# Storing the small gate rows of an mLSTM kernel from another engine's queue

## The chip, the cores and the metric

The kernel runs on one core of a Trainium2 chip. The time is device time of one execution in microseconds (us). The kernel before took 461.69 us, the median of three runs (461.58 to 464.37). The engines are named PE (TensorE, matrix products; PEld is its weight load), DVE (VectorE), ACT (ScalarE), POOL (GpSimd) and SP (SyncE, which only issues transfers). ScalarE and GpSimd can issue transfers too; a queue is named SPq or ACTq after its engine.

## The reference

An mLSTM cell over batch 4, 8 heads, 768 time steps and head size 40, whose output, read as 3072 tokens of 320, goes through an up product, a sigmoid-GELU and a down product.

```python
for t in range(S):
    m_new = np.maximum(f_gate[:, :, t] + m, i_gate[:, :, t])
    f_stab = np.exp(f_gate[:, :, t] + m - m_new)
    i_stab = np.exp(i_gate[:, :, t] - m_new)
    m = m_new
    C = f_stab * C + i_stab * outer(v_t, k_t)
    n = f_stab * n + i_stab * k_t
    y[:, :, t] = sigmoid(o_gate[:, :, t]) * (C @ q_t) / np.maximum(np.abs(n @ q_t), 1.0)
...
h = x @ w_in                                   # x: (3072, 320), w_in: (320, 2048)
g = h * (1.0 / (1.0 + np.exp(-1.702 * h)))
out = (g @ w_out).astype(np.float32)           # w_out: (2048, 320)
```

## The kernel before, in words

The sequence is cut into six chunks `w` of 128 steps. Within a chunk the recurrence is unrolled into attention-like products over 128 x 128 masked weights, plus a state that is carried from chunk to chunk. The program writes out the order of every engine by hand; each engine runs its instructions in that order and waits by semaphores.

From the second chunk on (`w` = 1 to 5) a chunk has two stages. In the first product, `up_fast(w, j)` for j = 0 to 7, a pair of the 16 column blocks of `w_in` is multiplied with the chunk's tokens: a Strassen-like scheme of seven products per pair, some of them shared through row banks. TensorE writes into four PSUM banks that `ps_m` hands out in turn and into the two double banks `p_a0` and `p_a1`. ScalarE copies one product to `parts` (L768), applies the activation to the pair before (L697) and copies one row bank to `g` (L746); VectorE adds up the rest (L769, L770, L782, L783); GpSimd adds the last part (L789). In the second product, `down_fast`, 14 blocks of products are multiplied with `w_out`, and between them stand the attention steps of chunk `w + 1`, at places given by the table `at` in `attention`: `columns`, `scale`, `decay`, `weights`, `carry` (the state, from k and v), `scores`, `values` and the `seam` steps, which bring the result into token order by way of memory.

The work around the change prepares chunk `w + 1` during the first product of chunk `w`:

- `load_squares` (L108), issued near the end of the second product before: k and q in square order, eight transfers by SyncE, 2.6 MB.
- `gates(w + 1)` behind the first pair (j = 0), on VectorE: the running sum of the forget gate (`f_run`), the running maximum (`m_run`), the stacked and swapped rows (`swapped`, in the tile named `f_run`) and the chunk's two decay ends (`both`). SyncE stores them to memory: three transfers to `m_row` (L304, L307), one to `st_row` (L330), one to `d_row` (L331). For `w + 1` = 1 it is GpSimd's queue instead, which `side_queue` chooses.
- `load(w + 1, "o")` (L122): the output gate into `eo`, 640 KB.
- `columns_in(w + 1)` behind the third pair (j = 2): SyncE reads the stored rows back in another layout into `raw` (four transfers from `st_row`, L354, and one from `d_row`, L356). `spread(w + 1)` reads `m_row` back to every partition into `wt` (L407). `load(w + 1, "vk")` (L120) loads v and k, three transfers each.
- `columns_turn` (behind the last pair) and the attention steps use `raw`, `wt`, `v_st` and `k_st`.

All these transfers of SyncE stand in one queue in the order given, and a store waits there until VectorE has made its rows. The `seam_out` stores of the second half are issued by ScalarE (L560). The row tiles in memory have two buffers, `m_run`, `swapped` and `st` have one.

Of the kernel before, what the change touches and what calls it, by code (L numbers as in the profile page):

```python
# [8 lines left out]
FP = mybir.dt.float32  # L9
# [17 lines left out]
def kernel(  # L27
# [14 lines left out]
    BH = B * H  # L42
# [10 lines left out]
    HL = L // 2  # L53
# [11 lines left out]
    rows = ctx.enter_context(tc.tile_pool(name="rows", bufs=2, space=bass.MemoryType.DRAM))  # L65
# [4 lines left out]
    V, A, G, T = nc.vector, nc.scalar, nc.gpsimd, nc.tensor  # L70
# [154 lines left out]
    m_at, ends = {0: m0}, {}  # L225
    cols, stacked, m_row, raw = {}, {}, {}, {}
# [51 lines left out]
    def side_queue(w):  # L278

        return G if w == 1 else nc.sync  # L280

    def gates(w):
        m = m_at[w]
        swapped = gate.tile([3 * BH, L], FP, bufs=1, name="f_run")
        f_run = swapped[0:BH, :]
        m_run = gate.tile([BH, L], FP, bufs=1, name="m_run")
        st = stacked[w] = gate.tile([3 * BH, L], FP, bufs=1, name="st")
        V.tensor_tensor_scan(out=f_run, data0=ones, data1=f_sb[w], initial=0.0, op0=OP.mult, op1=OP.add)
        a = st[0:BH, :]
        V.tensor_tensor(out=a, in0=i_sb[w], in1=f_run, op=OP.subtract)  # L290
        if w == 0:
            room = work.tile([L, H, D1], FP, tag="u", name="room").rearrange("p h d -> p (h d)")
            neg, part = room[0:BH, 0:L], room.bitcast(BF)[0:BH, 2 * L:3 * L]
            V.tensor_tensor(out=neg, in0=f_run, in1=i_sb[w], op=OP.subtract)
            split(G, a3, neg, neg, part)
        V.tensor_tensor_scan(out=m_run, data0=ones, data1=a, initial=m, op0=OP.mult, op1=OP.max)
        if w == 0:

            room = work.tile([L, H, D1], FP, tag="u", name="room").rearrange("p h d -> p (h d)")
            left, part = room[0:BH, 0:L], room.bitcast(BF)[0:BH, 2 * L:3 * L]  # L300
            split(V, m3, m_run, left, part)
        else:
            to = m_row[w] = rows.tile([2, BH, HL], FP, name="m_row")
            side_queue(w).dma_start(out=to[:, 0::2].rearrange("n h t -> h n t"),  # L304
                              in_=m_run[0::2].rearrange("h (n t) -> h n t", t=HL))
            for n in range(2):
                side_queue(w).dma_start(out=to[1 - n, 1::2], in_=m_run[1::2, n * HL:(n + 1) * HL])  # L307
        end = m_run[:, L - 1:L]
        if w + 1 < NW:
            m_at[w + 1] = gate.tile([BH, 1], FP, name="m_end")  # L310
            V.tensor_tensor(out=m_at[w + 1], in0=f_run[:, L - 1:L], in1=end, op=OP.add)

        mid = m_run[:, HL - 1:HL]
        for x, (old, new) in enumerate(((m, mid), (mid, end)) if w else ((m, end),)):
            t = slice(x * HL, x * HL + HL) if w else slice(0, L)
            V.tensor_scalar(out=st[BH:2 * BH, t], in0=m_run[:, t], scalar1=old, scalar2=None, op0=OP.subtract)
            V.tensor_scalar(out=st[2 * BH:3 * BH, t], in0=a[:, t], scalar1=new, scalar2=-1.0, op0=OP.subtract,
                            op1=OP.mult)
        if w:
            for x in range(2):  # L320
                V.tensor_scalar(out=swapped[:, x * HL:(x + 1) * HL], in0=st[:, (1 - x) * HL:(2 - x) * HL], scalar1=odd,
                                scalar2=None, op0=OP.mult)
            V.scalar_tensor_tensor(out=swapped, in0=st, scalar=even, in1=swapped, op0=OP.mult, op1=OP.add)
            both = ends[w] = gate.tile([BH, 2], FP, name="both")
            V.tensor_tensor(out=both[:, 0:1], in0=m, in1=mid, op=OP.subtract)
            V.tensor_tensor(out=both[:, 1:2], in0=mid, in1=end, op=OP.subtract)
            st_row = rows.tile([L // 32, 3 * BH, 32], FP, name="st_row")
            d_row = rows.tile([BH, 2], FP, name="d_row")
            stacked[w] = st_row, d_row
            side_queue(w).dma_start(out=st_row.rearrange("n k t -> k n t"), in_=swapped.rearrange("k (n t) -> k n t", t=32))  # L330
            side_queue(w).dma_start(out=d_row, in_=both)  # L331

    def slot(i, x):

# [23 lines left out]
    def columns_turn(w):  # L358
        c = cols[w] = gate.tile([L, 4 * BH], FP, name="cols")
        V.transpose(out=c[:, 0:3 * BH].rearrange("p (k h) -> p k h", h=BH),  # L360
                    in_=raw[w][:, 0:3 * BH].rearrange("p (k t) -> p k t", t=32))
# [232 lines left out]
    def wait_for(x):  # L594

        G.tensor_copy(out=mark[0:x.shape[0]], in_=x[:, 0:1])
# [212 lines left out]
    def weight_sums(n):  # L809
        out, a, b = ((t1, w01, w00), (t2, w11, t1), (w01, w11, w01), (t4, w10, t2))[n]  # L810
        G.tensor_tensor(out=out, in0=a, in1=b, op=OP.subtract)
# [60 lines left out]
    def run(calls):  # L872
        for f, *args in calls:
            f(*args)
# [62 lines left out]
    for w in range(NW):  # L937
        more = w + 1 < NW
        if w == 0:
            for j in range(NF // 2):  # L940
                if j % 2 == 0:
                    ahead, behind = converted[j // 2]
                    run([(convert, p) for p in ahead] + [(fetch, p) for p in fetched.get(j // 2, ())])
                    up(w, j, lambda: run([(columns_turn, 1) if p is None else (convert, p) for p in behind]))
                if j == 6:
                    load(1, "o")
                if j == 1:
                    wait_for(w_in_sb[:, 1, 512:1024])
                    scale(0, 1)
                    load(1, "v")  # L950
                if j < B and j % 2:
                    carry(0, (j // 2,))
                if j == 3:
                    masks()
                    gates(1)
                    columns_in(1)
                if j == 4:
                    spread(1)
                    load_squares(1, "q")
                if j >= B:  # L960
                    transposes(1, j - B)
        else:
            token_sums(w)
            for j in range(NF // 2):
                up_fast(w, j)
                if more and j == 0:
                    gates(w + 1)
                    load(w + 1, "o")
                    if w == 1:
                        wait_for(ends[w + 1])  # L970
                if w == 1 and j < 2:
                    weight_sums(j + 2)
                if more and j == 2:
                    columns_in(w + 1)
                    spread(w + 1)
                    load(w + 1, "vk")
                if more and j:
                    for n in ((0, 2), (), (4,), (6, 1, 3), (5, 7), (), ())[j - 1]:
                        block_transposes(w + 1, n)
                if more and j == 7:  # L980
                    columns_turn(w + 1)
                if 2 <= j < 6:
                    hidden_difference(w, j - 2)
                if j >= 6:
                    hidden_sums(w, (j - 6,), G)
            gelu_fast(w, NF // 2 - 1)
            hidden_sums(w, (2, 3), V)
        side = attention(w + 1) if more else {}
        if w == 0:

            blocks = [(lambda b=b, n=n: down(w, b, n)) for n0 in (0, 2) for b in range(B) for n in (n0, n0 + 1)]
        else:
            blocks = down_fast(w, 0) + down_fast(w, 1)
        for i, block in enumerate(blocks):
            if w == 0 and i in (0, 4, 5):
                convert((17, 18, 19)[max(i - 3, 0)])
            if w + 2 < NW and i == (6 if w == 0 else 0):
                load_gates(w + 2)
            if w + 2 < NW and i == 13:
                load_squares(w + 2, "kq" if w else "k")  # L1000
            if w == 0 and i == 15:
                load_squares(w + 2, "q")
            block()
            run(side.get(i, []))
            if w == 0 and i == 3:
                for n in (1, 3, 5, 7):
                    block_transposes(1, n)
            if w == 0 and i == 6:
                wait_for(wt[1, 0][:, 0, 0, :])
                weight_sums(0)  # L1010
                weight_sums(1)
            if w == 0 and i in (11, 13):
                input_sums(slice(0, 4) if i == 11 else slice(4, 8))
# [30 lines left out]
```

## Time and profile before

| | |
|---|---|
| median of three runs | 461.69 us |
| profiled execution | 463.3 us, of which span 461.6 us |
| granted TensorE clock | 1.000 |
| first products of `w` = 1 to 5 start at | about 112, 182, 254, 325, 396 us |
| second products of `w` = 1 to 5 start at | about 143, 214, 286, 357, 428 us |
| busy in 254 to 286 us (first product, `w` = 3) | PE 32.0, DVE 27.7, ACT 14.5, POOL 15.1; DMA share 0.91 |
| busy in 286 to 325 us (second product, `w` = 3) | PE 38.8, DVE 29.9, ACT 12.7, POOL 11.6; DMA share 0.39 |
| share of the chain that ended last | PE 75%, DVE 11%, ACT 4%, SPq 4%, DMA 3% |

"L304" is line 304 of the kernel. In a timeline a row has start and length in us, engine, line, operation, the tile written and the tile read, and the number of instructions merged; in brackets stands the idle time before it and what ended it. For transfers the length is that of the issue on its queue, not of the transfer; the time to landing is given apart. The DMA share is the mean busy share of the core's 16 DMA engines, and can go above 1 where packets overlap.

### The profile page before, as it was taken

How to read it: one execution, taken by the hardware profiler on the slowest of the kernel's cores; microseconds unless marked ns; L12 is line 12 of the kernel's file. 1: busy time of each engine (PE TensorE's matmuls, PEld its weight loads, DVE VectorE, ACT ScalarE, POOL GpSimd, SP SyncE). 2: the span in 40 equal slices, each digit the busy share in tenths (PEclk: the TensorE clock that was granted, in tenths of full speed). 3: DMA queues.
4: the chain of work that ended last, by engine and by line, in shares of the span. 5: the costliest groups of instructions: out<-in, count | busy, mean ns of one | idle time of the engine just before them, and what ended most of it. 6: DMA issues, size and time to landing. Idle time of an engine off the chain costs nothing.

```text
span 461.6 us, 12375 instructions
## 1 busy us (share of the span) xinstructions
PE 452.8 (98%) x5071; PEld 386.5 (84%) x5071; DVE 350.9 (76%) x738; ACT 186.0 (40%) x433; POOL 162.7 (35%) x155
## 2 busy tenths in 40 slices
PE   8999999999999999999899999999999999999996
PEld 6777877775779999779899779999888999787996
DVE  6788998899988876889786888787788767554622
ACT  5686779100546600546700354900264810164100
POOL 5101318130677500266700167610157710146200
PEclk9999999999999999999999999999999999999999
DMA  8999999038969044959224979315989505000000
GB/s 165 186 289 195 251 234 221 5 67 186 179 138 122 3 102 115 193 79 174 36 61 109 195 117 165 50 37 122 176 130 156 76 18 141 28 1 1 1 28 30
DMA packets 135561, 52.87 MB, mean 115 GB/s; under 512 B 101984, under 2 KB 131632, under 8 KB 135504
## 3 DMA queue, kind: packets, MB, share of 16 engines
q1 hardware_dynamic: 127136, 50.27, 56.0%
q10 hardware_dynamic: 8048, 1.66, 1.8%
q8 instruction: 40, 0.66, 0.7%
q0 software_dynamic: 320, 0.15, 0.2%
q14 instruction: 17, 0.14, 0.1%
HBM read 44.52 MB, written 7.54 MB: 113 GB/s over the span
## 4 chain that ended last, share of the span: by engine, by line
PE 75%; DVE 11%; ACT 4%; SPq 4%; DMA 3%; issue 2%; DVEq 0%; ACTq 0%
PE p_out L852 30%; PE p_h L729 16%; PE p_a L729 6%; PE p_h L631 5%; PE p_h L708 4%; PE p_a L708 3%; SPq L120 2%; PE p_a L507 2%; DMA st_row<-f_run 2%; PE p_a L515 2%; PE p_a L463 2%; PE p_a L605 2%; ACT wt L439 2%; PE p_h L640 1%; PE p_a L390 1%
## 5 line engine op out<-in xcount | busy, mean ns | idle before, releaser
L789 POOL TENSOR_TENSOR g<-g,parts 128x512 f32<-128x512 f32 x30 | 38.2, 1274 | 184.7 <-ACT g L746 175.9
L768 ACT COPY parts<-p_h 128x256 f32<-128x256 f32 x40 | 14.9, 372 | 164.6 <-PE p_h L729 159.5
L852 PE MATMUL p_out<-w_out_sb,g 128*128 128x160 f32 x480 | 68.9, 300 | 0.0
L852 PEld LDWEIGHTS p_out<-w_out_sb,g 128*128 128x128 f32 x480 | 66.4, 190 | 0.5
L697 ACT ACTIVATE g<-g 128x512 f32<-128x512 f32 x80 | 47.7, 629 | 23.8 <-DVE g L783 18.8
L857 DVE TENSOR_TENSOR o_sb<-o_sb,p_out 128x160 f32<-128x160 f32 x70 | 21.4, 317 | 43.6 <-PE p_out L852 43.0
L852 PE MATMUL p_out<-t_sb,s 128*128 128x160 f32 x320 | 47.1, 300 | 0.0
L729 PE MATMUL p_h<-xT,w_in_sb 128*128 128x256 f32 x160 | 45.4, 386 | 0.0
L852 PEld LDWEIGHTS p_out<-t_sb,s 128*128 128x128 f32 x320 | 44.4, 190 | 0.2
L729 PE MATMUL p_h<-t_x,s_in 128*128 128x256 f32 x160 | 41.2, 380 | 0.2 <-DVE t_x L684 0.2
L439 ACT ACTIVATE wt<-wt,cols 128x64 f32<-128x64 f32 x160 | 38.8, 333 | 0.1
L729 PEld LDWEIGHTS p_h<-xT,w_in_sb 128*128 128x128 f32 x160 | 29.4, 190 | 9.8 <-issue 6.3
L798 PE MATMUL p_out<-w_out_sb,g 128*128 128x320 f32 x128 | 35.7, 436 | 0.0
L729 PEld LDWEIGHTS p_h<-t_x,s_in 128*128 128x128 f32 x160 | 30.2, 190 | 4.8 <-DVE t_x L684 0.6
L798 PEld LDWEIGHTS p_out<-w_out_sb,g 128*128 128x128 f32 x128 | 23.9, 190 | 9.6
L769 DVE TENSOR_TENSOR t_x<-p_h,parts 128x256 f32<-128x256 f32 x40 | 17.0, 425 | 16.8 <-ACT g L697 8.7
L631 PE MATMUL p_h<-xT,w_in_sb 128*128 128x256 f32 x128 | 29.6, 384 | 0.0
L631 PEld LDWEIGHTS p_h<-xT,w_in_sb 128*128 128x128 f32 x128 | 23.6, 190 | 5.3 <-issue 2.4
L820 POOL TENSOR_TENSOR g<-g 128x512 f32<-128x512 f32 x20 | 25.5, 1276 | 0.0
L443 POOL TENSOR_SCALAR_AFFINE_SELECT wt<-wt 64x1024 f32<-64x1024 f32 x20 | 23.4, 1170 | 5.4 <-ACT wt L439 4.7
L852 PE MATMUL p_out<-w_out_sb,s 128*128 128x160 f32 x160 | 23.8, 302 | 0.0
L852 PE MATMUL p_out<-t_sb,g 128*128 128x160 f32 x160 | 23.8, 302 | 0.0
(221 smaller groups left out, 892.4 us busy)
## 6 DMA issues: line engine op xcount, KB each, us to landing
q_sq<-in_q_dram SPq DMA_DIRECT2D x20, 320.0 KB, 10.2
wt<-m_row SPq DMA_DIRECT2D x20, 256.0 KB, 5.6
k_sq<-in_k_dram SPq DMA_DIRECT2D x16, 320.0 KB, 6.3
out_dram<-o_sb SPq DMA_DIRECT2D x24, 160.0 KB, 1.9
eo<-in_o_gate_dram SPq DMA_DIRECT2D x5, 640.0 KB, 8.5
bits<-in_moe_w_in_dram SPq DMA_DIRECT2D x6, 512.0 KB, 11.4
q_sq<-x_row SPq DMA_DIRECT2D x10, 256.0 KB, 2.9
v_st<-in_v_dram SPq DMA_DIRECT2D x14, 160.0 KB, 5.9
```

Source lines behind the costliest of these rows:

```text
L439: A.activation(out=x[:, h, :], in_=x[:, h, :], func=AF.Exp, scale=-1.0, bias=cols[w][:, c * PH + h:c * PH + h + 1])
L443: G.affine_select(out=r, in_=r, compare_op=OP.is_ge, fill=0.0, base=0, pattern=[[0, PH], [1, HL]], channel_multiplier=-1)
L631: T.matmul(ph[j][i][:, t], w_in_sb[:, c, f * 128:(f + 1) * 128], x[:, c, t], start=(first and c == 0 and n == 0), stop=(not first and c == ...
L697: A.activation(out=gs[w, j][:, i, :], in_=gs[w, j][:, i, :], func=AF.Gelu_apprx_sigmoid)
L708: T.matmul(row[:, t], w_in_x[r, j, :], xT[w][r, 2].rearrange("p b t -> p (b t)")[:, t], start=(start and h == 0), stop=(not start and h == ...
L729: T.matmul(out, a, x[n], start=start, stop=stop)
L769: V.tensor_tensor(out=u2, in0=p56[:, right], in1=y[:, left], op=OP.add)
L789: G.tensor_tensor(out=g0, in0=g0, in1=u, op=OP.add)
L798: T.matmul(po, gs[w, f // 2][:, f % 2, b * L:(b + 1) * L], w_out_sb[:, f, :], start=(f == 0), stop=(f == NF - 1))
L820: G.tensor_tensor(out=a10, in0=a00, in1=a10, op=OP.subtract)
L852: T.matmul(po, a(f), b[:, f, :], start=(f == 0), stop=(f == NH - 1))
L857: V.tensor_tensor(out=dst, in0=x, in1=po, op=OP.add)
```

## The change

From `w + 1` = 2 on, the five stores of the small rows are no longer issued by SyncE inside `gates`, behind the first pair (j = 0). The tiles are kept in `held`, and a new function `gates_out` issues the five stores from ScalarE behind `up_fast(w, 1)`, the second pair, ahead of the read-back, which stays on SyncE behind the third pair. The data, the layouts and the number of transfers stay as they were; for `w + 1` = 1 the stores stay with GpSimd.

```diff
+    held = {}
+
+    def maxima_out(w, m_run, engine):
+        to = m_row[w]
+        engine.dma_start(out=to[:, 0::2].rearrange("n h t -> h n t"), in_=m_run[0::2].rearrange("h (n t) -> h n t", t=HL))
+        for n in range(2):
+            engine.dma_start(out=to[1 - n, 1::2], in_=m_run[1::2, n * HL:(n + 1) * HL])
+
+    def columns_out(w, swapped, engine):
+        st_row, d_row = stacked[w]
+        engine.dma_start(out=st_row.rearrange("n k t -> k n t"), in_=swapped.rearrange("k (n t) -> k n t", t=32))
+        engine.dma_start(out=d_row, in_=ends[w])
+
+    def gates_out(w):
+        m_run, swapped = held[w]
+        maxima_out(w, m_run, A)
+        columns_out(w, swapped, A)
+
     def gates(w):
...
-            to = m_row[w] = rows.tile([2, BH, HL], FP, name="m_row")
-            side_queue(w).dma_start(out=to[:, 0::2].rearrange("n h t -> h n t"),
-                              in_=m_run[0::2].rearrange("h (n t) -> h n t", t=HL))
-            for n in range(2):
-                side_queue(w).dma_start(out=to[1 - n, 1::2], in_=m_run[1::2, n * HL:(n + 1) * HL])
+            m_row[w] = rows.tile([2, BH, HL], FP, name="m_row")
+            if w == 1:
+                maxima_out(w, m_run, G)
...
-            side_queue(w).dma_start(out=st_row.rearrange("n k t -> k n t"), in_=swapped.rearrange("k (n t) -> k n t", t=32))
-            side_queue(w).dma_start(out=d_row, in_=both)
+            if w == 1:
+                columns_out(w, swapped, G)
+            held[w] = m_run, swapped
...
                 if w == 1 and j < 2:
                     weight_sums(j + 2)
+                if more and j == 1:
+                    gates_out(w + 1)
                 if more and j == 2:
                     columns_in(w + 1)
                     spread(w + 1)
```

## The prediction, made before the changed kernel ran

> **What bounds the kernel now.** I read the busy times first, then what TensorE waits for, then the chain of waits in order of time from 182 us on, then SyncE's queue and ScalarE's order of time around the stores that move.
>
> ```profile
> PE 452.8 (98%) x5071; PEld 386.5 (84%) x5071; DVE 350.9 (76%) x738; ACT 186.0 (40%) x433; POOL 162.7 (35%) x155
> ```
>
> TensorE is busy 452.8 of 461.6 us. Of the 8.8 us left, 5.6 lie between 22 and 460 us (busy 432.44 of 438.00). No edit to transfers can win more than that. Its own waits, of which these two can be traced to a transfer:
>
> ```profile
> PE p_a L605 <- DMA k_st<-in_k_dram: 0.6, 1, 0.6
> PE p_a L463 <- DVE state L616: 0.6, 1, 0.6
> ```
>
> Both lie in one place, at 223.0 and 228.5 us, in the second product of the chunk that starts at 182 us. The chain of waits (start, length, what) leads from there back to a store that moves:
>
> ```profile
> 192.29 9.55 DMA st_row<-f_run
> ...
> 201.91 1.86 SPq L354
> ...
> 209.03 4.51 SPq L120
> ...
> 219.41 4.12 DMA k_st<-in_k_dram
> ```
>
> The stacked rows need 9.55 us to land; only then does SyncE issue their read-back, the spread of the maxima, v and k, and TensorE's `carry` meets the last piece of k at 223.57. SyncE's queue ahead of that (start, length, issues):
>
> ```profile
> 180.88 2.08 SPq L108 DMA_DIRECT2D k_sq<-in_k_dram  x4
> 183.06 5.59 SPq L108 DMA_DIRECT2D q_sq<-in_q_dram  x4
> 188.74 1.48 SPq L861 DMA_DIRECT2D out_dram<-o_sb  x1
> 190.32 0.61 SPq L304 DMA_DIRECT2D m_row<-m_run  x1
> 190.98 1.22 SPq L307 DMA_DIRECT2D m_row<-m_run  x2
> 192.29 0.53 SPq L330 DMA_DIRECT2D st_row<-f_run  x1
> 194.05 0.32 SPq L331 DMA_DIRECT2D d_row<-both  x1
> 196.66 0.40 SPq L122 DMA_DIRECT2D eo<-in_o_gate_dram  x1
> ```
>
> Two gaps matter, before `d_row` and before `eo`. SyncE's waits put both down to `q_sq` loads (L331 3.7 us over 4 chunks, L122 9.2 us over 5), whose data neither reads. Counted in this queue, `d_row` is the eighth issue after the second `q_sq` load and `eo` the eighth after the third: an issue waits for the landing of the one eight before it. ScalarE at the point where the stores go (behind the copy at 192.32):
>
> ```profile
> 192.32 0.56 ACT L746 COPY g<-p_h 128x512 f32<-128x512 f32 x1
> 193.90 0.59 ACT L746 COPY g<-p_a 128x512 f32<-128x512 f32 x1 [1.01 <-PE p_a L729]
> 194.38 0.38 ACT L768 COPY parts<-p_h 128x256 f32<-128x256 f32 x1
> 194.65 1.16 ACT L697 ACTIVATE g<-g 128x512 f32<-128x512 f32 x2
> 195.70 0.37 ACT L768 COPY parts<-p_h 128x256 f32<-128x256 f32 x1
> ```
>
> It is idle 1.02 us there (192.88 to 193.90).
>
> **Part 1, what leaves SyncE.** Five issues a chunk in four chunks (those starting at 112, 182, 254, 325 us): 1.92 us for the three `m_row`, 0.58 for `st_row`, 0.37 for `d_row` with their gaps, 2.87 in all. TensorE never waits for these issues as such. `eo` then follows the output store at 190.3 instead of 196.66, its eighth predecessor being a `k_sq` load long landed. `eo` has no reader before 226 us, so that alone is worth nothing.
>
> **Part 2, what ScalarE gets.** The same five issues, behind the second pair. Their data are ready (DVE writes `both` at 191.69, ScalarE arrives at 192.88), so no wait for DVE is added. ScalarE's own issues on its queue, the four `x_row` and `x_rest` stores at 170.59, took 1.40 and 1.08 us for pairs, 0.62 each, so five cost about 2.9, as on SyncE. But `d_row` is now the eighth issue after the third `q_sq` load (q, out, `eo`, three `m_row`, `st_row`, `d_row`), and if ScalarE's issues count with SyncE's it waits for the landing that `eo` waits for today: 123.60, 196.66, 268.22, 339.66 in the four chunks. The trace shows no such wait on ScalarE; its cost is bounded by nothing and by those times. I take the wait, because ScalarE's `x_row` stores each have a semaphore instruction among them beyond their data's.
>
> Behind `d_row` on ScalarE stand the third pair's row copy (L746), its L768 copy, the gelus of the second pair and the fourth pair's L768 copy. That last one frees the PSUM bank into which TensorE multiplies as the second product of the fifth pair. ps_m hands out four banks in turn. In the 182 chunk it ends at 196.07 and TensorE gets there at 198.44, so the cover is 2.37 us, plus ScalarE's 1.02 idle: 3.39 us may pass free. With the row copy at s, the L768 copy ends at s + 2.17. By chunk:
> - 112: ScalarE arrives 121.99, the issues end at 124.86; the copy ends at 127.05 (the GpSimd wait at 124.95 is absorbed), needed at 127.51: no stall.
> - 182: arrives 192.88, `d_row` goes at 196.66 and ends 196.98; copy ends 199.17, needed 198.44: 0.73.
> - 254: arrives 265.04, `d_row` 268.22 to 268.54; copy ends 270.73, needed 270.59: 0.14.
> - 325: arrives 335.98, `d_row` 339.66 to 339.98; copy ends 342.17, needed 341.55: 0.62.
>
> Together 1.5 us. DVE's half of the pair moves with it: its L770 of the fourth pair goes from 198.33 to about 200.7, and TensorE needs that bank at 200.17 plus the 0.73. It fits. DVE's 0.93 us wait for TensorE at 202.3 then takes up most of the delay.
>
> **Part 3, when the rows land.** Now behind 2.6 MB of k and q in one queue; after, in a queue of their own beside them. Nearest rows: ScalarE's stores land in 2.5 to 2.9 us in a quiet stretch, and the first chunk's stores by GpSimd's queue, beside a DMA share of 0.84 to 0.90, in 3.3 (`m_row`), 5.5 (`st_row`) and 6.0 (`d_row`). I take the latter: `st_row` at 194.8 + 5.5 = 200.3 (201.84 now), `d_row` at 202.7, against 205.28 when its read-back is issued now. SyncE's first read-back is stretched to 1.86 us by `eo` draining ahead of it; an earlier `eo` shortens that. So v and k come some 2 to 3 us sooner. Worth: the 0.57 us wait for k, and of the 0.62 us behind it half, since GpSimd's `vw` (220.19, held by v) also starts sooner: 0.9 us, at most 1.2, at least 0. No other chunk has a wait to win.
>
> **Sum.** On the profiled execution (463.3 us, of which 461.6 span): 463.3 - 0.9 + 1.5 = 463.9. It lay 1.6 above the median, 461.69, so 462.3 us.
>
> **A rule against it.** ScalarE and SyncE issued at the same moment at 172.6 us (0.54 and 0.6 us) and at 244.5 (0.56 and 0.62), no longer than either does alone. The Trainium skill, Perfetto Trace Analysis, "DMA Instruction — HWDGE (DVE, Sync)", says that the descriptor generator is shared by two sequencers and locked by one while it generates, and that this lock wait counts in the issue's length. By the rows the five issues keep their 2.9 us and the sum stands at 462.3. By the rule ScalarE's issues could queue behind `eo`'s, and the time would go to that of the second rival, some 482. The rows are of small transfers, so they don't settle it.
>
> **Rivals.**
> 1. *The cover holds*: no landing is waited for on ScalarE, the five issues take 2.9 us, under 3.39, and only the gain is left: 461.69 - 0.9 = 460.8; with the whole 1.2, 460.5, less 0.1 for the distance of the two close runs (461.58 and 461.69) 460.4. For it: the idle time and the L768 slack in every chunk. Against: the two gaps in SyncE's queue.
> 2. *ScalarE is held behind `eo`* (slower). On SyncE the issue after `eo` ends 7.1 us after it (196.66 to 203.77). If that holds another engine's issues too, the first `m_row`, with `eo` issued at 190.3, is done between 197.4 and, counting that q drains until about 197 (the DMA share falls from 1.14 to 0.54 there) and `eo`'s 640 KB follow, 200.5; the five end at 199.7 to 202.8, the L768 copy 2.2 later, 3.5 to 6.6 past TensorE's need. Times four chunks: 14 to 26 us, 476 to 488, middle 482. It decides from 3.39 us of ScalarE's time on. For it: such blocked issues (5.59 us for four, 4.51 for one) stand on SyncE. Against: the two overlaps above.
> 3. *Each issue is slow beside full DMA engines*: at the longest ScalarE issue seen, 0.94 us, five take 4.95 with gaps and the stalls are 1.6 in each chunk, 6.4 in all: 461.69 - 0.9 + 6.4 = 467.2.
> 4. *The rows land later than now*: the transfers stop (DMA share 0.03 or less) about 1 us ahead of `carry` in the 254 chunk (294 against 294.87) and 2 us in the others (150 against 151.79, 364 against 365.84), in the 182 chunk they don't. A read-back 3 us late costs 3 + 2 + 1 + 1 = 7: 468.7. It needs `d_row` to take over 11 us to land, as long as the slowest row store today.
>
> **How the numbers follow.** One per cent, 4.6 us, is about what a measurement of this kernel tells from no change. The forecast, stalls of 0.5 to 3 us against the gain, has 0.47 (own range 461 to 464); rival 1 0.25; rival 2 0.12; rival 3 0.10; rival 4 0.04; a gain over 1%, 0.02, for which the idle of TensorE hardly leaves room. Within 1% stand the first two and the lower end of rival 3: 0.74; slower 0.24. The range takes in the forecast and rivals 1 and 3: 460.4 to 467.5, leaving 0.18 out.
>
> **What would show it.** ScalarE's queue with five issues after the copy at about 192.9 and a gap ahead of the fifth; TensorE idle 0.1 to 0.8 us ahead of the second product of the fifth pair in the chunks at 182, 254 and 325, put down to the L768 copy; `eo` at about 190 and the read-back at about 200; no wait for `k_st` at L605. An `m_row` issue on ScalarE longer than 3 us would make rival 2 right; no idle at the fifth pair, rival 1. The forecast is wrong if the median is below 461 or above 464.

## The result, and the profile after

The changed kernel takes 463.39 us (median of 21 executions, 461.84 to 466.73), the kernel before, run beside it, 462.20 us (median of 21, 461.58 to 464.37). The ratio is 1.0032 with a 95% interval of 1.0020 to 1.0045: slower by 1.2 us between the medians and 1.5 us by the ratio, within one per cent. (In the experiments, too, a ratio is to the kernel before, run beside that version.) The profiled execution of the changed kernel took 463.11 us, of which 461.4 us are span, at a granted clock of 1.00. Lines below the new functions carry numbers 17 higher than before (L463 is now L480, L605 is L622, L746 is L763).

The busy times of the changed kernel, and what its TensorE waits for (us in total, times, longest), answer to the two views shown first:

```profile
PE 453.0 (98%) x5071; PEld 386.7 (84%) x5071; DVE 351.7 (76%) x738; ACT 185.2 (40%) x433; POOL 162.6 (35%) x155
```

```profile
PE p_a L480 <- DVE state L633: 1.0, 1, 1.0
```

The counts of instructions are those of before and each busy time is within 1 us of it, and no wait is put down to an L785 copy (the stall that was forecast) or to `k_st`. ScalarE's timeline in the chunk that starts at 182 us, where the stores now stand:

```profile
191.97 0.64 ACTq L286 DMA_DIRECT2D m_row<-m_run  x1
192.05 0.56 ACT L763 COPY g<-p_h 128x512 f32<-128x512 f32 x1
192.65 1.24 ACTq L288 DMA_DIRECT2D m_row<-m_run  x2
193.99 0.53 ACTq L292 DMA_DIRECT2D st_row<-f_run  x1
194.61 0.44 ACTq L293 DMA_DIRECT2D d_row<-both  x1
195.09 0.59 ACT L763 COPY g<-p_a 128x512 f32<-128x512 f32 x1 [2.48 <-DMA m_row<-m_run]
```

Five issues follow each other without a gap and hold ScalarE until 195.09; `d_row` waits for nothing. All five first products take as long as before, from the first matmul of a stage to the first of the next: 33.67 us in the chunk at 112 us (its first matmul stands at 109.07), 31.84 to 31.88 in the others. SyncE's timeline of the same chunk shows what was not forecast:

```profile
180.61 2.08 SPq L108 DMA_DIRECT2D k_sq<-in_k_dram  x4
182.80 12.96 SPq L108 DMA_DIRECT2D q_sq<-in_q_dram  x4
195.87 0.43 SPq L878 DMA_DIRECT2D out_dram<-o_sb  x1
196.40 0.39 SPq L122 DMA_DIRECT2D eo<-in_o_gate_dram  x1
196.88 8.87 SPq L371 DMA_DIRECT2D raw<-st_row  x4
```

The four `q_sq` loads took 5.59 us to issue before; now it is 12.96, and `eo` stands at 196.40, not at 190. SyncE's waits in this chunk name the reasons:

```profile
SPq L108 <- DMA k_sq<-in_k_dram: 6.4, 2, 5.2
SPq L108 <- DMA m_row<-m_run: 5.1, 1, 5.1
```

A load of q has no use for an `m_row` store. The semaphores in the trace explain it: each transfer signals one of eight when it lands, SyncE's and ScalarE's transfers take turns at the same eight, in the order planned when the program was built, and an issue waits until the former user of its semaphore has landed. In that order ScalarE's stores now stand ahead of three of the four `q_sq` loads. The second and third `q_sq` loads have the semaphores of the last two `k_sq` pieces and wait for these; the fourth has that of ScalarE's first `m_row` store, which lands at 195.44, and is issued at 195.46 (186.94 before).

The rows themselves gained, as the list of transfers in 180 to 222 us shows (KB each, median us from issue to landing); the kernel before:

```profile
m_row<-m_run SPq DMA_DIRECT2D x2, 4.0 KB, 10.3
st_row<-f_run SPq DMA_DIRECT2D x1, 48.0 KB, 9.6
```

and the changed kernel:

```profile
st_row<-f_run ACTq DMA_DIRECT2D x1, 48.0 KB, 2.0
m_row<-m_run ACTq DMA_DIRECT2D x2, 4.0 KB, 2.7
```

They land by about 199.4 (`d_row`: issue at 194.61, 4.8 us), but the issue of the first read-back, behind `eo`, ends only at 204.33 (203.77 before): the last 320 KB of q and the 640 KB of `eo` are now in front of it. The last piece of k is issued at 218.74.

The chain of waits in this chunk (start, length, what) no longer passes through any transfer:

```profile
222.52 1.61 PE p_a L622 x128
...
226.52 0.50 DVE state L633
227.02 1.01 DVE state L600
228.03 0.02 issue
228.05 0.51 DVE state L633
228.56 0.04 issue
228.60 1.16 PE p_a L480 x64
```

TensorE waits 1.01 us for VectorE's state, and VectorE for nothing but itself. Why its decay product (L600) takes a full microsecond there is the last question of the experiments.

### The profile page after: what moved, and what is told of

It is laid out like the page before. It is cut to its first block, busy times and chain, and to the rows that moved or that the text cites. A ratio compares the mean times of both kernels' runs of the same rounds, so it can differ in the third digit from the quotient of the medians.

```text
span 461.4 us, 12376 instructions
## 1 busy us (share of the span) xinstructions
PE 453.0 (98%) x5071; PEld 386.7 (84%) x5071; DVE 351.7 (76%) x738; ACT 185.2 (40%) x433; POOL 162.6 (35%) x155
## 4 chain that ended last, share of the span: by engine, by line
PE 82%; DVE 9%; DMA 5%; SPq 2%; issue 1%; ACT 1%; DVEq 0%
PE p_out L869 33%; PE p_h L746 19%; PE p_a L746 7%; PE p_h L725 4%; PE p_a L725 4%; PE p_h L648 3%; DMA q_sq<-in_q_dram 2%; PE p_a L524 2%; PE p_a L532 2%; PE p_a L622 2%; PE p_a L480 1%; DMA bits<-in_moe_w_out_dram 1%; SPq L92 1%; PE p_a L407 1%; DVE qT L415 1%
## 5 line engine op out<-in xcount | busy, mean ns | idle before, releaser
L785 ACT COPY parts<-p_h 128x256 f32<-128x256 f32 x40 | 14.9, 372 | 164.4 <-PE p_h L746 164.4
L746 PE MATMUL p_h<-xT,w_in_sb 128*128 128x256 f32 x160 | 45.4, 386 | 0.0
L746 PE MATMUL p_h<-t_x,s_in 128*128 128x256 f32 x160 | 41.2, 380 | 0.2 <-DVE t_x L701 0.2
L746 PEld LDWEIGHTS p_h<-xT,w_in_sb 128*128 128x128 f32 x160 | 29.4, 190 | 9.8 <-issue 6.3
L746 PEld LDWEIGHTS p_h<-t_x,s_in 128*128 128x128 f32 x160 | 30.2, 190 | 4.8 <-DVE t_x L701 0.6
L609 POOL TENSOR_TENSOR vw<-v_st,cols 128x656 f32<-128x656 f32 (+1 forms) x13 | 16.7, 1295 | 22.9 <-ACT cols L388 12.5
L854 DVE TENSOR_TENSOR s<-g,s 128x256 f32<-128x256 f32 x40 | 24.1, 641 | 0.0
```

Source lines behind the costliest of these rows:

```text
L746: T.matmul(out, a, x[n], start=start, stop=stop)
L854: V.tensor_tensor(out=s2, in0=hidden(w, j + 4, 0)[:, :, c], in1=s2, op=OP.subtract)
```

## The experiments

Two theories came first. Theory 1: the loss comes from SyncE's side, v and k arrive later. Theory 2: it comes from ScalarE, which the five issues hold. A scale for both is the length of the stages, from the first matmul of one to the first of the next; the second products of the chunks at 112, 182 and 254 us take 39.1 us when nothing is late, the one at 325 us 38.61.

**GpSimd's queue in place of ScalarE's.**

```diff
-        maxima_out(w, m_run, A)
-        columns_out(w, swapped, A)
+        maxima_out(w, m_run, G)
+        columns_out(w, swapped, G)
...
+                    gates_out(w + 1)
...
-                if more and j == 1:
-                    gates_out(w + 1)
```

> The same five stores from GpSimd's queue, directly behind the gates. Theory 1 (late loads: in the changed kernel the last q_sq load is issued 8.5 us later, at 195.46 instead of 186.94, since it waits for the landing of a store by ScalarE, and v and k come about 1 us later in three of four chunks): here no q_sq load waits for a store, it is issued near 187 again, the last k load by 219 or earlier, and the time is 1 to 2 us under the changed kernel, 461.3 to 462.3. Theory 2 (ScalarE's 2.9 us hold delays the sums behind it): also under it, since ScalarE is free, but GpSimd now holds its own addition of the second pair about 2 us, so 462 to 463.5. The order of SyncE's issues tells whether the late load is gone, the time alone tells little.

463.60 us, ratio 1.0031 (1.0019 to 1.0043), above what either theory gave. The `q_sq` loads aren't held and the last k of the 182 chunk is issued 33.3 us after the chunk's start (36.9 in the changed kernel); the second products stand at 39.28, 39.11, 39.10 and 38.61. But the first product at 112 us takes 35.21 us in place of 33.67: there GpSimd also has weight sums to do (L828, two of 2.9 us between 123.36 and 130.34), and they now stand behind its five issues (120.58 to 123.34). A loss as large as the change's, but in another place: that first product is 1.54 us longer, behind GpSimd's issues (read from the timeline, not tested apart), and no q load is held.

**The stores on SyncE, but behind the second pair** (the diff is against the changed kernel).

```diff
-        maxima_out(w, m_run, A)
-        columns_out(w, swapped, A)
+        maxima_out(w, m_run, nc.sync)
+        columns_out(w, swapped, nc.sync)
```

> The five stores stay on SyncE, but behind the eo load (the place of the changed kernel, ScalarE untouched). Theory 1: no q_sq load is held, but the small rows land behind eo's 640 KB, at about 204 instead of 202, the read-back and with it v and k come 1 to 3 us later, and carry waits: 463 to 467. Theory 2: ScalarE is free, so no slower than before: 461.5 to 462.5.

468.05 us, ratio 1.0110 (1.0079 to 1.0142), above the 463 to 467 of theory 1. The first `m_row` issue takes 8.68 us behind `eo` (193.65), the last k goes at 223.44, and TensorE's waits name k itself:

```profile
PE p_a L622 <- DMA k_st<-in_k_dram: 3.4, 8, 0.8
PE p_a L480 <- DVE state L633: 1.3, 2, 0.7
```

So late rows do reach TensorE, with second products of 42.62, 41.24 and 41.08 us in the profiled execution, the slowest of six (469.89 us). Part of the 42.62 is a granted clock of 0.62 from 154 to 158 us, not waiting.

**`eo` behind v and k, in the changed kernel and in the kernel before.** Both move the same line:

```diff
-                    load(w + 1, "o")
...
                     load(w + 1, "vk")
+                    load(w + 1, "o")
```

> The changed kernel with the eo load behind the loads of v and k. ScalarE does what it does in the changed kernel. Theory 1: the read-back is no longer stretched by eo (7.45 us at 196.88), v and k are issued 3 to 6 us earlier, no carry waits for k: 461.0 to 462.3, at least 1 us under the changed kernel. Theory 2: no change, 463.4. Both: eo lands near 227 in the second chunk, where ScalarE's tanh may wait up to 2 us without cost.

> The kernel before with the eo load behind the loads of v and k. Theory 1: v and k come 2 to 4 us earlier in every chunk, so the waits at 223.0 and 228.5 us go: 461.0 to 461.6 against 462.2. Theory 2 says nothing of v and k beyond that; no change or the same gain.

With the stores on ScalarE, 462.25 us, ratio 1.0003 (0.9995 to 1.0012): the whole loss of the change is gone, with ScalarE's five issues where they were. The `q_sq` loads still take 12.79 us to issue; the read-back behind them now takes 2.96 us instead of 8.87, and the last k goes at 213.53. This speaks against theory 2, and shows that the late q loads cost time only while `eo` too stands in front of the read-back. The same move in the kernel before gives 462.20, ratio 1.0001 (0.9992 to 1.0009): no gain, where one was expected. The waits of 0.57 and 0.62 us that the prediction meant to win don't stand in the second profile of that kernel (below).

**ScalarE held by copies.** The kernel before, with eleven or twenty-two extra copies, no transfer moved:

```diff
+                if more and j == 1:
+                    for _ in range(11):
+                        A.copy(out=spare_out, in_=ident.unsqueeze(1).to_broadcast([128, 2, 128]))
```

> The kernel before (stores on SyncE) with eleven extra ScalarE copies of 128x256 behind the second pair in the four chunks, estimated at 2.9 us from the 0.26 us between two such copies' ends in the profile: ScalarE is held as long as by the five issues, and no transfer moves. Theory 1 (ScalarE's hold is covered, 1.02 us of idle and 2.37 us until the fourth pair's copy is needed; the loss of the change comes from SyncE's transfers alone): 462.0 to 462.6, TensorE's first products at 31.84 us. Theory 2 (the hold itself costs): 463 to 464, the loss of the change.

> The same with twenty-two copies, about 5.8 us of hold. If the cover is the 3.39 us that the prediction worked out, each of the four chunks stalls by 5.8 - 3.4 = 2.4 us in its first product (34.2 instead of 31.84): 471 to 473. If the cover is larger, as would follow if TensorE's next block could go ahead, 462 to 466.

Both expectations mis-sized the copy: it takes 0.43 us each, not 0.26. Eleven gave 466.97 us, ratio 1.0105 (1.0092 to 1.0119). ScalarE's and then TensorE's timeline around the hold:

```profile
193.15 0.57 ACT L747 COPY g<-p_h 128x512 f32<-128x512 f32 x1
193.62 4.78 ACT L976 COPY spare_out<-ident 128x256 f32<-128x256 f32 x11
198.30 0.58 ACT L747 COPY g<-p_a 128x512 f32<-128x512 f32 x1
```

```profile
199.21 0.70 PE L730 MATMUL p_h<-xT,w_in_sb 128*128 128x256 f32 x2 [0.20 <-ACT parts L769]
200.19 0.70 PE L730 MATMUL p_h<-xT,w_in_sb 128*128 128x256 f32 x2 [0.29 <-DVE parts L771]
```

The row copy starts 5.15 us behind the second pair's copy, where it was 1.58 before (193.90 and 192.32): it is 3.57 us late. The stage grows by 1.21 us (33.05 against 31.84), so 2.36 us passed free, against the 2.37 us of slack that the prediction worked out at the fourth pair's copy. In the changed kernel the same distance is 195.09 - 192.05 = 3.04 us, the row copy 1.46 late: covered, with 0.9 us to spare, since the issues begin beside the copy ahead of them. Theory 2 falls.

Twenty-two copies gave 492.91 us, ratio 1.0661 (1.0644 to 1.0679). The row copy is 8.37 us late (210.34 and 200.39, less 1.58), 6.0 more than the slack, but each stage grows by 7.6 to 8.3 us. The 4-us windows of this run (window: length, then busy us and instructions of PE, PEld, DVE, ACT, POOL, the granted clock, DMA share, GB/s) have the rest:

```profile
204.00:208.00 4.00, 2.25 (x11) 1.64 (x9) 0.00 (x0) 3.71 (x10) 0.00 (x0) 1.00 0.56 79
208.00:212.00 4.00, 0.76 (x2) 0.50 (x2) 0.68 (x2) 3.84 (x10) 0.00 (x0) 0.70 0.82 134
212.00:216.00 4.00, 4.00 (x11) 3.05 (x10) 3.83 (x8) 2.41 (x7) 2.60 (x3) 0.50 0.48 115
```

TensorE stands still for 4.99 us from 206.25 on, and comes back at half clock. The Trainium skill says the same in "TensorE: Matmul & The Clock Gate", section "What's actually happening": after an idle window of about 3.4 us the clock falls to half. The rows of this run don't test that bound closely; another run's, in the last section, don't fit it.

**The false wait of the q loads taken away.** Issuing `k_sq` one block earlier puts two of the four `q_sq` loads ahead of ScalarE's stores in the planned order, from the 182 chunk on; now `eo` has the semaphore of the first `m_row`:

```diff
-                load_squares(w + 2, "kq" if w else "k")
+                load_squares(w + 2, "q" if w else "k")
+            if w and w + 2 < NW and i == 12:
+                load_squares(w + 2, "k")
```

> The changed kernel with the four k_sq loads of the next squares issued one step earlier in the second product, so that two q_sq loads come before ScalarE's stores in the planned order and the other two get semaphores whose earlier users are an output store and the first q_sq load, in the chunks from 182 on; eo now has that of ScalarE's first m_row store. Theory 1 (the fourth q_sq load waited for ScalarE's m_row store, and this made all behind it late): the q_sq loads are issued within some 6 us as before the change, no wait for m_row ahead of them, the last k_st issue comes 0.5 to 2 us earlier than in the changed kernel: 462.0 to 462.7. Theory 3 (the late q_sq loads are harmless, and the rows' own landing sets v and k): as the changed kernel, 463.2 to 463.6.

462.64 us, ratio 1.0015 (1.0000 to 1.0029), at the upper end of what theory 1 said. SyncE's timeline of the 182 chunk (which starts 1.80 us later than in the changed kernel's profile):

```profile
182.47 6.67 SPq L108 DMA_DIRECT2D q_sq<-in_q_dram  x4
190.43 0.37 SPq L878 DMA_DIRECT2D out_dram<-o_sb  x1
195.66 0.39 SPq L122 DMA_DIRECT2D eo<-in_o_gate_dram  x1
198.83 2.78 SPq L371 DMA_DIRECT2D raw<-st_row  x4
```

The loads take 6.67 us instead of 12.96, the last k goes 4.7 us earlier counted from the chunk's start, and all second products from there on are at their floor (39.10, 39.10, 38.61), although `eo` now waits 4.8 us for the `m_row` store. Only the chunk at 112 us, whose order is still that of the change, lies over it: 40.10.

**The same in the first chunk too.** `k_sq` and `q_sq` of the chunk before it one and two blocks earlier:

```diff
-                load_squares(w + 2, "q" if w else "k")
-            if w and w + 2 < NW and i == 12:
+                load_squares(w + 2, "q" if w else "")
+            if w + 2 < NW and i == 12:
                 load_squares(w + 2, "k")
-            if w == 0 and i == 15:
+            if w == 0 and i == 13:
                 load_squares(w + 2, "q")
```

> As the run before with the k_sq loads one step earlier, and the loads of the first such chunk (second product that ends near 109 us) moved ahead too: k_sq at its block 12 in place of 13, q_sq at its block 13 in place of 15, so that in the chunk starting at 112 us no q_sq load has a semaphore of ScalarE's stores or of a k_sq load behind them. Theory 1: its last k_st issue returns from 148.6 to 144 to 146.5 us, its second product from 40.1 to 39.1 us, every other stage stays as it was: 462.0 to 462.4, no difference from the kernel before. Theory 3 (what is left of the loss in that run is not the q_sq loads): 462.6 as there, and the product stays at 40.1.

478.38 us, and no test of anything: `q_sq` still held tokens of the second chunk, which VectorE turns from it only later (L593), so part of that chunk was computed from rows of q, and TensorE waited 15.3 us for the turned tokens. Instead, starting from the run before it, the stores of that chunk were left on SyncE, and only those of the three later chunks go by ScalarE (`columns_out` is changed like `maxima_out`):

```diff
-            if w == 1:
-                maxima_out(w, m_run, G)
+            if w <= 2:
+                maxima_out(w, m_run, G if w == 1 else nc.sync)
...
-                if more and j == 1:
+                if w >= 2 and more and j == 1:
                     gates_out(w + 1)
```

> As the run with the k_sq loads one step earlier, but the stores of the chunk that starts at 112 us stay on SyncE's queue at their old place (so no change of the order there), and only those of the three later chunks go by ScalarE. Theory 1: the one product of that run that lay over its floor (40.1 us, the second one of this chunk) returns to 39.1, every other stays: 462.0 to 462.4, no difference from the kernel before, with three of four chunks' stores on ScalarE. If a loss of 0.5 us or more is left, theory 1 lacks a part: 462.6 or more.

462.08 us, ratio 1.0001 (0.9992 to 1.0009). The second products are 39.10, 39.10, 39.12 and 38.61: nothing is left of the loss, with three of four chunks' stores on ScalarE. Nor is there a gain: no version tried was faster than the kernel before, whose stages stand at their floors in its second profile (below). Theory 1 holds, and theory 3 of the expectations, that the late q loads are harmless, falls for the change as it stands.

**Second looks at both kernels.**

> The kernel before once more, for a second profiled execution. If the two waits of 0.6 us at 223.0 and 228.5 us belong to every execution, they are here too, and the second product of the third chunk takes 40.3 us; if they belonged to the one execution that was profiled (463.3 us, over the median), all second products from there on take 39.1 us or 38.6, and the time is 462.2.

> The changed kernel once more, for a second profiled execution. Theory 1: the second and third q_sq loads again wait for k_sq landings and the fourth for the first m_row, in the chunks from 182 on; the sum over the second products lies 0.5 to 2 us over the floor of 39.1 and 38.6 us a stage, in which chunk varies; 463.2 to 463.7. If v and k are late in the same chunk by the same amount as in the first profile, the time they take is fixed by the order, not by the execution.

The kernel before: 462.76 us in one execution, second products 39.09, 39.10, 39.10 and 38.61, no wait for k or the state. The 40.3 us of its first profile belonged to that execution (463.3 us, over the median). The changed kernel: 463.35 us, ratio 1.0023 (1.0009 to 1.0037), profiled in an execution of 465.95 us with second products of 41.78, 40.16, 39.55 and 38.61, 4.2 us over their floors where at most 2 was expected. In both profiles q holds v and k back; which chunks pay, and how much, differs. Why v was late in the first profile of the kernel before stays open. Counted from the chunk's start, GpSimd starts `vw` in the 182 chunk at 36.5 us when it waits for its columns, and later when it waits for v:

| profiled run | `vw` starts | the two decays of VectorE | second product |
|---|---|---|---|
| before, second look | 36.53 | 0.66, 0.49 | 39.10 |
| after with `eo` behind v and k | 36.51 | 0.66, 0.49 | 39.10 |
| after with `k_sq` earlier | 36.53 | 0.66, 0.49 | 39.10 |
| after | 37.64 | 1.38, 1.08 | 40.10 |
| after, second look | 37.96 | 1.27, 0.83 | 40.16 |
| before, first profile | 38.09 | 1.24, 0.83 | 40.30 |

**Why a microsecond.** GpSimd's and VectorE's timelines in the second look at the kernel before:

```profile
219.28 2.75 POOL L592 TENSOR_TENSOR vw<-v_st,cols 128x656 f32<-128x656 f32 x2 [2.17 <-ACT cols L371]
223.73 2.34 POOL L443 TENSOR_SCALAR_AFFINE_SELECT wt<-wt 64x1024 f32<-64x1024 f32 x2
```

```profile
225.76 0.66 DVE L583 TENSOR_TENSOR state<-state_mid,cols 128x328 f32<-128x328 f32 x1
226.53 0.50 DVE L616 TENSOR_TENSOR state<-p_a,state 128x328 f32<-128x328 f32 x1
226.94 0.49 DVE L583 TENSOR_TENSOR state<-state_mid,cols 128x328 f32<-128x328 f32 x1
```

and in the changed kernel:

```profile
219.48 2.71 POOL L609 TENSOR_TENSOR vw<-v_st,cols 128x656 f32<-128x656 f32 x2 [3.30 <-DMA v_st<-in_v_dram]
223.72 2.35 POOL L460 TENSOR_SCALAR_AFFINE_SELECT wt<-wt 64x1024 f32<-64x1024 f32 x2
226.53 2.49 POOL L460 TENSOR_SCALAR_AFFINE_SELECT wt<-wt 64x1024 f32<-64x1024 f32 x2 [0.46 <-ACT wt L456]
```

```profile
225.03 1.38 DVE L600 TENSOR_TENSOR state<-state_mid,cols 128x328 f32<-128x328 f32 x1
226.52 0.50 DVE L633 TENSOR_TENSOR state<-p_a,state 128x328 f32<-128x328 f32 x1
226.94 1.08 DVE L600 TENSOR_TENSOR state<-state_mid,cols 128x328 f32<-128x328 f32 x1
```

With v on time, the first pair of selects is almost done when VectorE's first decay comes, and the second pair begins behind the second decay. With v late, GpSimd is about 0.9 us behind, and both decays meet a select. The first decay ends about 0.35 us after GpSimd's pair in both kernels (226.42, and the pair at 226.07), whether that makes it 0.66 or 1.38 us long: it waits for the select to end. The sum at L633, which reads one operand from PSUM, is not touched (0.50). The Trainium skill, "SBUF — State Buffer", section "SBUF: two separate sides", says that VectorE, for an operation with two inputs in SBUF, and GpSimd take turns at a shared pair of ports, locked for a whole instruction; these rows agree.

k has a part in it too. `carry` in the changed kernel, and below it in the second look at the kernel before:

```profile
222.45 1.68 PE L622 MATMUL p_a<-vw,k_st 64*40 64x41 f32 x128
```

```profile
223.38 1.45 PE L605 MATMUL p_a<-vw,k_st 64*40 64x41 f32 x128
```

In the changed kernel the last piece of k lands at 222.67, when `carry` has begun, and `carry` takes 0.23 us longer, too little to be listed as a wait. VectorE's first decay comes 0.2 us later for it, counted from the second product's start, and so falls behind the start of the second select instead of ahead of it. In the 254 chunk of the same profile `vw` is later still (37.93), but the decay begins 0.10 us ahead of the select (297.04 and 297.14) and takes 0.49 us; that second product is 39.36. In the second look at the changed kernel v alone was enough: in its first chunk `carry` takes its usual time, v lands at 148.12 and `vw` starts at 148.28, 1 us late, and the decays take 1.39 and 1.27 us.

To test the block without a late transfer, GpSimd got two idle products ahead of `vw` in the kernel before:

```diff
+            if 2 <= w <= 4 and c == 0:
+                for _ in range(2):
+                    G.tensor_tensor(out=spare_vw, in0=ident.unsqueeze(1).to_broadcast([128, 2, 128]),
+                                    in1=cols[w][:, 2 * BH:2 * BH + 2].unsqueeze(2).to_broadcast([128, 2, 128]), op=OP.mult)
```

> The kernel before (no store moved, no transfer's order changed) with two idle GpSimd products of 128x256 (about 0.65 us each, half of the 1.28 us of 128x512 in the profile) ahead of vw in the second products of the chunks at 112, 182 and 254 us, so that vw, GpSimd's share of the decay and its first pair of selects run some 1.2 us later, as they do in the changed kernel when v lands late; v and k themselves are on time. Theory 4 (the last link: late selects of GpSimd block VectorE's two decay products, which read two operands from SBUF, L583 here, until they are done): these take 1.2 to 1.5 and 0.8 to 1.1 us in place of 0.66 and 0.49, TensorE waits about 1 us for the state, the three second products take 40.0 to 40.3 us in place of 39.1, and the time is 465.0 to 466.2. Its rival (TensorE is late only because v and k are late; GpSimd has a microsecond of slack there): 462.0 to 462.6, the products at 39.1.

462.74 us, ratio 1.0011 (1.0003 to 1.0020): a loss, but 0.5 us and not 3. The three second products take 39.33, 39.33 and 39.34. `vw` starts 1.47 us late (38.00 from the chunk's start, later than in the changed kernel), the decays take 0.72 and 0.83:

```profile
224.99 0.72 DVE L584 TENSOR_TENSOR state<-state_mid,cols 128x328 f32<-128x328 f32 x1
225.81 0.50 DVE L621 TENSOR_TENSOR state<-p_a,state 128x328 f32<-128x328 f32 x1
226.23 0.83 DVE L584 TENSOR_TENSOR state<-state_mid,cols 128x328 f32<-128x328 f32 x1
```

Taken singly, the selects here stand at 224.22 to 225.36, 225.43 to 226.71, 226.78 to 228.06, and the decays end at 225.71 and 227.06, again 0.35 us behind a select's end; the sum at 225.81 runs inside a select and keeps its 0.50 us. The first decay came 0.37 us before one ended, and had little to wait for; in the changed kernel it came at 225.03, just after the second select had begun (224.93), and waited for nearly all of it. So the block is shown with no transfer late, and its price isn't set by how late GpSimd is but by where in a select the decay falls: between nothing and most of a select per decay. That theory 4's 1 us a chunk failed here is this phase: late v moves the selects, late k moves the decays, and this run moved the selects alone, by 1.47 us where `vw` was 1.1 us late in the changed kernel. The full microsecond was only observed with late transfers, not made without them.

## Why the prediction held in its number, and where it failed

The forecast was 462.3 us, within 460.4 to 467.5 and within one per cent; 463.39 came out. Of its terms, -0.9 and +1.5 us, neither occurred, and the loss that did occur has no term in its sum. So the number held by luck, helped by a range that also took in two rivals.

- *Part 1, `eo` at 190.3*: wrong, and this is the step that failed. It went at 196.40. The prediction saw that an issue waits for the landing of the one eight before it, and used that for `d_row` and `eo`; but it counted in the order in which transfers had been issued before, with the `q_sq` loads ahead of the stores, and left those loads where they were. That ScalarE's issues count with SyncE's, which it took without a wait to show it, was right. The eight turn in the planned order, and there ScalarE's stores had moved ahead of q. The wait that was feared on ScalarE (`d_row` for a q load) came the other way round, on SyncE (a q load for `m_row`).
- *Part 2, ScalarE*: the five issues took 3.1 us where 2.9 were forecast, and the slack of 2.37 us was right, as the eleven copies show (2.36). The stalls of 1.5 us did not occur, since `d_row` waited for nothing.
- *Part 3, the rows and what follows*: the rows land even sooner than was taken (2.0 us for `st_row`, 5.5 taken), yet the read-back gained nothing, because q and `eo` came in front of it. The gain of 0.9 us was read from waits in one profiled execution of before; a second look and the move of `eo` show none to win. In their place the change lost 1.2 us, by making v and k late: v is late in the 182 chunk in both profiles of the changed kernel and in one of two of the kernel before.
- *Rival 1* (the cover holds) was right about ScalarE and wrong about the time. *Rival 2* (ScalarE's issues held behind `eo`) did not occur: `eo` never went ahead of them in the changed kernel. In the run with `k_sq` earlier it did: there `eo` goes at 195.66, and ScalarE issues `st_row` and `d_row` right behind it (195.78 and 196.41) in 0.54 and 0.50 us, not held. What they would do with q still on its way was not tried. *Rival 3* (slow issues) did not occur: 0.44 to 0.64 us each in the 182 chunk. *Rival 4* named the right path, v and k late, for the wrong reason: the rows landed earlier, not later.

The points at which the prediction said it would fail (below 461 or above 464) were not reached; its own tests in the profile were better: `eo` not at 190, no idle at the fifth pair.

## What to carry to other kernels

Before a transfer is moved to another queue, count whose landing each later issue will wait for, in the program's new order: completion semaphores that several queues share can tie a large load to a small store that it has nothing to do with. A wait that is to be won must stand in more than one profiled execution; here the second look at the kernel before would have removed the gain term. And when TensorE waits on VectorE with no transfer in its chain of waits, look at what GpSimd runs beside it: a late transfer that makes an engine with slack slip by a microsecond can cost as much on another.

## What was not expected of the hardware

- A VectorE product with two SBUF operands takes 0.49 us alone and up to 1.47 us beside GpSimd's selects; where it is held it ends about 0.35 us after a select, while a sum with a PSUM operand keeps its 0.50 us.
- The granted clock fell after a small stop too. In the second look at the changed kernel TensorE waited 1.25 us for the state at 156.3 us, less than the idle window of about 3.4 us cited above, and the 4-us windows around it read:

```profile
153.00:157.00 4.00, 3.34 (x80) 3.03 (x79) 3.90 (x5) 3.61 (x12) 3.22 (x4) 1.00 0.01 4
157.00:161.00 4.00, 3.41 (x73) 3.35 (x74) 3.97 (x8) 0.00 (x0) 1.01 (x1) 0.72 0.01 4
161.00:165.00 4.00, 4.00 (x139) 3.78 (x139) 0.79 (x3) 0.00 (x0) 0.00 (x0) 0.86 0.13 43
```

  That second product took 41.78 us, 2.7 over its floor, of which the wait is less than half. A wait of 1.01 us in the changed kernel's first profile left the clock at 1.00. So a stop well under that window can be followed by a lower clock here; what decides it stays open.
